# A routed feed-forward behind normalised attention: the last token chunk's dense product on two column halves, with the issue order drawn up anew

## The chip, the cores and the metric

The kernel runs on one core of a Trainium2 chip. The metric is the device time of one execution in microseconds; the profiled execution is recorded by the hardware profiler. The engines are named as in the profile: PE (the matrix engine, with PEld for its weight loads), DVE (vector), ACT (scalar), POOL (gpsimd) and SP (here only a queue that issues DMAs).

## The reference

Eight batches, 12 heads, 448 tokens, head size 64. Attention with normalised q and k gives x, one row of 768 for each of the 3584 tokens; each row then takes a dense feed-forward and one of eight experts.

```python
q_n, k_n = rmsnorm(q, g_q), rmsnorm(k, g_k)
attn = softmax(q_n @ k_n.T / 8)
x = (attn @ v) as rows [3584, 768]

y_dense = maximum(x @ w1_dense, 0) @ w2_dense      # 768 -> 512 -> 768
logits = x @ w_gate                                # 8 experts
e = argmax(logits); gate = softmax(logits)[e]
y_moe = gate * (maximum(x @ w1[e], 0) @ w2[e])
out = y_dense + y_moe
```

## The kernel before

The attention works in 24 groups of four heads, three groups to a batch, so a batch is one round of the steady state. Per group there are seven score steps (`scores`, L339 on PE, two heads at a time on two row halves of 64; then one exponential of 128x896 on ACT, L341), the product with v (`attend`, L357), transposes of q and k (`transposes`, L304), their copies out of PSUM on DVE (qT L317, kT L323 and L325), the division (L390, L384), the transposes of x (`xtrans`, L398) and the gate logits (L416). The norms go through DVE statistics (L272), small ACT steps (m L279, ln L285, r L287) and POOL (ss L281, then four multiplications xn, L293). POOL also casts v (`values`, va, L258), issues the weight loads (L629) and the scatters.

When a batch of x is done, its 448 tokens are taken in four chunks of 128 columns that begin at 0, 128, 256 and 320 (`QC`), so that the first 64 rows of the last chunk repeat the third one's. For each chunk m, `dense` multiplies x by `wd1` (six matmuls of 128x512, L572), `relu` (L576, ACT) writes the result as bf16 beside x in the token's record, and `scatter` (L477, POOL) sends the 128 records to a slot in DRAM. The slots come from `choose`, `ranks` (L463) and `places`: `places` multiplies the ranks by the one-hot choice (at, L471), sums over eight experts (sf, L473) and adds `inval` (L474), which is zero but for the first 64 rows of the last chunk, where it is so large that the scatter skips the repeated rows.

From about 206 us on the kernel is in its tail: records are read back sorted by expert, transposed by DMA (`turn`, on SP), in tiles of 128 tokens. Each tile takes `gemm1` (L762), a transpose (`htrans`, L777), and `gemm2` (L790 for the dense second matrix, L801 for the expert's), a copy out (L814) and a scatter of the output (L817). A few tiles hold two experts with 64 tokens each. Their matmuls work on two column halves of the array (L758 with L759, L801 with L806): 64 stationary columns each, the two results in partitions 0 to 63 and 64 to 127. The dense products of batches 6 and 7 partly lie between the first tiles.

The order on every engine is fixed by hand. The dictionary `AT` gives each step of the steady state a place in units of score steps; all steps are sorted by it and issued in that order, and each engine works through its share in order. `AT["pro"]` and `AT["tail"]` list the start and the tail step by step; `AT["we"]` gives places to weight loads by number (17 is the first matrix of the last expert), and `AT["wt"]` can put such a load ahead of a tile of the tail.

Of the kernel before, what the change touches and what calls it, by code (L numbers as in the profile page):

```python
# [17 lines left out]
AT = dict(  # L18
    p00=[-0.862, 1.524, -1.092],
    p01=[1.061, 2.118, -0.075],  # L20
    d0=[1.097, 3.011, 0.182],
    p10=[3.67, 3.575, 2.886],
    p11=[4.686, 3.605, 4.04],
    d1=[7.184, 5.02, 4.162],
    xt=[11.96, 12.342, 14.734],
    xe=[12.836, 12.616, 15.279],
    tr=[2.755, 1.399, 2.327],
    tq=[3.163, 3.396, 3.158],
    tk=[3.197, 4.021, 5.092],
    va=[-0.884, 1.723, 1.392],  # L30
    st=[(0.275, 0.047), (-0.382, 0.169), (-0.631, 0.101)],
    me=[2.591, 2.79, 3.569],
    no=[3.342, 3.796, 4.041],
    nm=[(7.457, 0.108), (4.843, 0.142), (5.124, 0.082)],
    kq='qk',
    lv=[-8.965, -4.183, -6.466],
    lq=[6.473, 4.67, 2.212],
    lk=[4.188, -0.439, 2.722],
    lo=[13.905, 13.666, 16.642],
    ch=(10.029, 0.135),  # L40
    ra=11.951,
    pl=(13.119, 0.051),
    ga=(10.595, 0.157),
    de=[(0, 0, [(11.866, 0, 4), (12.291, 4, 6)], 13.185, 14.228),
        (1, 1, [(14.061, 0, 2), (14.676, 2, 6)], 14.828, 20.5),
        (2, 0, [(20.56, 0, 6)], 20.943, 27.29), (3, 0, [(26.48, 0, 6)], 28.824, 32.5)],
    we={1: 16.0, 2: 122.0, 3: 20.0, 4: 32.85, 5: 45.7, 6: 58.55, 7: 71.4, 8: 84.25, 9: 97.1,
        10: 109.95, 11: 122.8, 12: 135.65, 13: 139.5, 14: 144.215, 15: 145.293, 16: 150.009, 17: 212.877, 18: 160.695},
    bl=24.0,
    wt={},  # L50
    el=(146.335, 0.654),
    s0=[-0.586, 0.455, 2.566],
    s1=[-2.814, 1.363, 3.272],
    s2=[0.964, 2.804, 2.08],
    s3=[0.9, 0.991, 3.16],
    s4=[3.908, 5.032, 3.847],
    s5=[5.085, 6.201, 1.162],
    s6=[5.915, 4.026, 6.263],
    pro=[('ld', 'k', 0), ('ld', 'q', 0), ('id',), ('ld', 'q', 1), ('gl',), ('co',),
# [23 lines left out]


@with_exitstack
def kernel(
# [73 lines left out]
    dbase = const.tile([P, 4], F32)  # L160
    inval = const.tile([P, 4], F32)
    oh = const.tile([P, B + 1, 5, E], BF16)
# [207 lines left out]
    def free(who):  # L370
        for p in [p for p in held if held[p] == who]:
            del held[p]
# [196 lines left out]
    def dense(b, m, bank, k0, k1):  # L569
        claim("0" if bank == 0 else "1 1r", ("de", b, m))  # L570
        for kk in range(k0, k1):
            seen(nc.tensor.matmul(W[:, bank], xTs[b][:, kk, QC[m]:QC[m] + P], wd1[:, kk],  # L572
                             start=(kk == 0), stop=(kk == KD - 1)), "W", "pe", bank)

    def relu(b, m, bank):
        seen(nc.scalar.activation(rb[b % 3][:, m, XH:GO].bitcast(BF16), W[:, bank], AF.Relu),  # L576
             "W", "act", bank)
        free(("de", b, m))
# [3 lines left out]
    def constants():  # L582
        nc.vector.memset(ones, 1.0)
        nc.vector.memset(onef, 1.0)
        nc.vector.memset(inval, 0.0)
        nc.vector.memset(inval[:D, 3:4], OOB)
        for e in range(E):
# [56 lines left out]
    def attention():  # L644
# [30 lines left out]
        for b in range(B):  # L675
            z = J * NB * (b + 1)
            put(at("ch", z, 0), ("ch", b), 8, lambda b=b: choose(b))
            put1(at("ra", z, 0), ("ra", b), ranks, b)
            put(at("pl", z, 0), ("pl", b), 3, lambda b=b: places(b))
# [283 lines left out]
```

## Time and profile before

| what | value |
|---|---|
| median of 3 runs | 355.06 us |
| lowest and highest of the 3 | 354.93, 364.9 us |
| the profiled execution's own time | 355.05 us |
| its span, first to last instruction | 353.4 us |
| busy: PE, DVE, ACT, POOL | 321.0, 220.2, 212.8, 203.5 us |
| granted TensorE clock, mean | 0.994 |

A busy PE includes the latency of its matmuls, so the pitch at which matmuls follow one another says more of its load than its busy share. In rows of the timeline a name such as L572 is the line in the kernel, then operation, tile written and tile read, shape and count; a bracket at the end gives the idle time of the engine just before and what ended it.

### The profile page before, as it was taken

To read this page: it belongs to the slowest core of one execution; us is meant where nothing else is said; L and a number is where in the kernel's file an instruction comes from. 1 tells how busy PE (TensorE), PEld (TensorE's weight loads), DVE (VectorE), ACT (ScalarE), POOL (GpSimd) and SP (SyncE) were. 2 spreads that over 40 slices of the span, in tenths; PEclk is the share of its full clock that TensorE was granted. 3 is DMA by queue.
4 is the path that set the end of the run, shared out by engine and by line. 5 is a ranking of instruction groups with operands and counts; after the bars stand their busy time and mean duration, and the time that the engine had idled before them with its cause. 6 is when DMAs were issued, how large, how long until landed. Compare 5 with 4: busy or idle time off the path is not lost.

```text
span 353.4 us, 11109 instructions
## 1 busy us (share of the span) xinstructions
PE 321.0 (91%) x4058; PEld 194.4 (55%) x4058; DVE 220.2 (62%) x801; ACT 212.8 (60%) x342; POOL 203.5 (58%) x282
## 2 busy tenths in 40 slices
PE   0498989999999999999998998999999999999991
PEld 0255655666565665666565565555555555555550
DVE  4978999989889888898987734362222222442321
ACT  2379998798898997988987733322233222332220
POOL 4476897697896987988989321555232222222321
PEclk9999999999999999999999999999999999999997
DMA  7996999999999999969999998999966666666312
GB/s 234 234 267 182 290 268 275 294 244 307 274 309 288 243 318 263 295 185 285 295 243 217 246 196 173 209 282 263 259 172 166 185 185 167 159 155 146 104 67 91
DMA packets 81817, 79.80 MB, mean 226 GB/s; under 512 B 48222, under 2 KB 73310, under 8 KB 81760
## 3 DMA queue, kind: packets, MB, share of 16 engines
q1 hardware_dynamic: 70672, 43.24, 49.0%
q0 software_dynamic: 11088, 35.80, 37.7%
q8 instruction: 36, 0.59, 0.7%
q14 instruction: 21, 0.17, 0.2%
HBM read 61.40 MB, written 24.07 MB: 242 GB/s over the span
## 4 chain that ended last, share of the span: by engine, by line
PE 21%; issue 19%; DMA 10%; POOL 6%; ACT 5%; POOLq 3%; DVE 2%; DVEq 0%; ACTq 0%
DMA out_dram<-xflat,tail 9%; PE W L572 7%; PE AV L357 5%; POOL out_dram L817 4%; ACT xflat L341 4%; PE sc L339 3%; POOLq L816 1%; DMA xflat<-records 1%; PE W L398 1%; PE W L304 1%; POOL xn L293 1%; POOLq L562 1%; PE mid L762 1%; PE yp L790 1%; PE AV L416 1%
## 5 line engine op out<-in xcount | busy, mean ns | idle before, releaser
L341 ACT ACTIVATE xflat<-sc 128x896 bf16<-128x896 f32 x168 | 144.6, 917 | 13.5 <-PE sc L339 12.2
L293 POOL TENSOR_TENSOR xn<-we,r 128x448 bf16<-128x448 f32 x92 | 83.9, 944 | 14.2 <-ACT r L287 6.9
L357 PE MATMUL AV<-va,xflat 128*128 128x65 bf16 (+1 forms) x1536 | 75.9, 195 | 1.7 <-issue 0.7
L814 DVE COPY xflat<-yp 128x768 f32<-128x768 f32 x29 | 27.7, 956 | 78.5 <-PE yp L801 68.6
L817 POOL DMA_INDIRECT out_dram<-xflat,tail x30 | 30.9, 1031 | 78.3 <-DVE xflat L814 64.3
L339 PE MATMUL sc<-qT,kT 64*128 64x448 bf16 x384 | 68.0, 366 | 7.2 <-ACT xflat L341 4.8
L357 PEld LDWEIGHTS <-xflat 128*128 128x128 bf16 (+1 forms) x1536 | 60.1, 97 | 25.4 <-issue 14.4
L272 DVE BATCH_NORM_STATS2 st<-we 128x6 f32<-128x128 f32 x336 | 69.8, 279 | 2.8 <-DMA we<-in_k_dram 2.8
L781 ACT COPY heT<-AV 128x512 bf16<-128x512 bf16 x27 | 15.8, 586 | 56.3 <-PE AV L777 56.3
L572 PE MATMUL W<-wd,xT 128*128 128x512 bf16 x192 | 47.5, 380 | 1.0 <-DVE kT L325 1.0
L477 POOL DMA_INDIRECT records<-rall,slot x32 | 33.3, 1040 | 25.4 <-DVE rall L450 7.3
L801 PE MATMUL yp<-we,heT 128*128 (+1 forms) x240 | 44.0, 326 | 0.0
L790 PE MATMUL yp<-wd,xflat 128*128 128x384 bf16 x240 | 43.9, 326 | 0.0
L384 DVE TENSOR_TENSOR rall<-AV,inv 128x256 bf16<-128x256 f32 x96 | 36.3, 420 | 2.0 <-DVE inv L390 0.3
L339 PEld LDWEIGHTS <-kT 64*128 64x128 bf16 x384 | 24.1, 95 | 22.8 <-issue 17.3
L762 PE MATMUL W<-we,xflat 128*128 x144 | 35.0, 379 | 0.7 <-issue 0.7
L790 PEld LDWEIGHTS <-xflat 128*128 128x128 bf16 x240 | 23.2, 98 | 18.9 <-issue 1.2
L767 ACT ACTIVATE hs<-W,tail 128x512 bf16<-128x512 f32 x27 | 18.6, 687 | 23.5 <-PE W L762 16.3
L801 PEld LDWEIGHTS <-heT 128*128 128x128 bf16 (+1 forms) x240 | 23.4, 99 | 15.6 <-issue 1.0
L576 ACT ACTIVATE rall<-W 128x512 bf16<-128x512 f32 x32 | 19.0, 597 | 19.5 <-PE W L572 19.4
L258 POOL CAST va<-we 128x448 bf16<-128x448 f32 x48 | 26.9, 590 | 0.0
L572 PEld LDWEIGHTS <-xT 128*128 128x128 bf16 x192 | 16.4, 97 | 19.0 <-issue 3.8
(132 smaller groups left out, 301.4 us busy)
## 6 DMA issues: line engine op xcount, KB each, us to landing
we<-in_moe_w_dram POOLq DMA_DIRECT2D x16, 768.0 KB
we<-in_q_dram SPq DMA_DIRECT2D x24, 448.0 KB
we<-in_k_dram SPq DMA_DIRECT2D x11, 896.0 KB
we<-in_v_dram SPq DMA_DIRECT2D x48, 128.0 KB
we<-in_v_dram SPq DMA_DIRECT2D x48, 96.0 KB
wd<-in_moe_w_dense_dram POOLq DMA_DIRECT2D x2, 768.0 KB
records<-rall POOLq DMA_DIRECT2D x8, 162.0 KB
we<-in_k_dram SPq DMA_DIRECT2D x2, 448.0 KB
```

Source lines behind the costliest of these rows:

```text
L272: return [lambda s=s: nc.vector.bn_stats(sts[g][:, "qk".index(name), s].rearrange("p h c -> p (h c)"), xin[name, g].rearrange("p h (s d) - ...
L293: (eng or nc.gpsimd).tensor_tensor(xn[name, g][:, :, hh], xin[name, g][:, hh].rearrange("p (s d) -> p s d", d=D), r[:, "qk".index(name), : ...
L339: nc.tensor.matmul(ps[:, hh, :S], kT[row, c:c + P], qT[row, r], start=(n == 0), stop=(n == len(mm) - 1), skip_group_check=True)
L341: nc.scalar.activation(x, ps[:, :, :S], AF.Exp, scale=scale)
L357: seen(nc.tensor.matmul(av[:, hh, m], exs[g, s][rows_, hh, QC[m]:QC[m] + P], va[rows_, s, hh, :De], start=(first and s == full[0] and m == ...
L384: seen(nc.vector.tensor_tensor(x[:, 2 * hh + r], av[:, hh, :, :D].rearrange("p m (a i) -> p m a i", a=2), inv[:, hh].unsqueeze(3).to_broad ...
L477: i = nc.gpsimd.indirect_dma_start(out=rec, out_offset=bass.IndirectOffsetOnAxis(ap=slot[b % 2][:, m:m + 1], axis=0), in_=rb[b % 3][:, m], ...
L572: seen(nc.tensor.matmul(W[:, bank], xTs[b][:, kk, QC[m]:QC[m] + P], wd1[:, kk], start=(kk == 0), stop=(kk == KD - 1)), "W", "pe", bank)
L762: got = [nc.tensor.matmul(he, xRs[t][:, kk], w, **args)]
L790: nc.tensor.matmul(yps[t][:, dd, :HD], xRs[t][:, KD + i], wd2[:, i, dd * HD:(dd + 1) * HD], start=(i == 0), stop=False, skip_group_check=True)
L801: done.append(nc.tensor.matmul(yp[:cut, dd, :HD], heTs[t][:, i, :cut], mats(t)[:, bass.ds(eregs[t], 1), 1, cols] .rearrange("p o f -> p (o ...
L817: i = nc.gpsimd.indirect_dma_start(out=out, out_offset=bass.IndirectOffsetOnAxis(ap=tail[:, t, 1:2], axis=0), in_=ys.rearrange("p a d -> p ...
```

## The change

Four things change. First, `dense` for the last chunk (m = 3) takes only the 64 new tokens as stationary columns, and computes the 512 outputs as two halves of 256, one on each column half of the array: twelve matmuls of 64x256 in place of six of 128x512. `relu` for that chunk becomes two activations of 64x256, which both write to partitions 64 to 127; the other 64 records of that chunk are zeroed once at the start. Second, `places` keeps `inval` as a ninth column of its product tile, so that one sum over nine columns writes the slot. Third, all numbers in `AT` are new, which moves steps on every engine. Fourth, weight load 17 leaves the list of the tail and goes ahead of tile 5 on POOL.

```diff
-    de=[(0, 0, [(11.866, 0, 4), (12.291, 4, 6)], 13.185, 14.228),
-        (1, 1, [(14.061, 0, 2), (14.676, 2, 6)], 14.828, 20.5),
-        (2, 0, [(20.56, 0, 6)], 20.943, 27.29), (3, 0, [(26.48, 0, 6)], 28.824, 32.5)],
+    de=[(0, 0, [(11.933, 0, 4), (12.358, 4, 6)], 12.949, 14.283), (1, 1, [(14.061, 0, 2), (14.379, 2, 6)], 14.828, 20.5), (2, 0, [(20.557, 0, 6)], 20.995, 27.068), (3, 0, [(26.48, 0, 6)], 28.938, 32.5)],
...
-    wt={},
+    wt={5: [17]},
...
-          ('g2', 0, 1), ('we', 17), ('tu', 2), ('de', 7, 2), ('re', 7, 2), ('se', 7, 2),
...
     def places(b):
         rk = W[:, 1, RK:].rearrange("p (m e) -> p m e", e=E)
-        at = sb.tile([P, 4, E], F32, tag="at", name="at")
-        sf = sb.tile([P, 4], F32, tag="sf", name="sf")
-        return [lambda: (seen(nc.vector.tensor_tensor(at, rk, oh[:, b, :4], ALU.mult), "W", "dve", 1),
-                         free(("ra", b))),
-                lambda: nc.vector.tensor_reduce(sf, at, AX.X, ALU.add),
-                lambda: nc.vector.tensor_tensor(slot[b % 2], sf, inval, ALU.add)]
+        at = ats[b % 2]
+
+        def found():
+            with nc.allow_low_precision(reason="whole numbers, at most one of them not zero"):
+                nc.vector.tensor_reduce(slot[b % 2], at, AX.X, ALU.add)
+
+        return [lambda: (seen(nc.vector.tensor_tensor(at[:, :, :E], rk, oh[:, b, :4], ALU.mult),
+                              "W", "dve", 1), free(("ra", b))), found]
...
         for kk in range(k0, k1):
-            seen(nc.tensor.matmul(W[:, bank], xTs[b][:, kk, QC[m]:QC[m] + P], wd1[:, kk],
-                             start=(kk == 0), stop=(kk == KD - 1)), "W", "pe", bank)
+            if m < 3:
+                seen(nc.tensor.matmul(W[:, bank], xTs[b][:, kk, QC[m]:QC[m] + P], wd1[:, kk],
+                                 start=(kk == 0), stop=(kk == KD - 1)), "W", "pe", bank)
+                continue
+            for h in range(2):
+                seen(nc.tensor.matmul(W[h * D:(h + 1) * D, bank, :F // 2], xTs[b][:, kk, S - D:],
+                                 wd1[:, kk, h * F // 2:(h + 1) * F // 2], start=(kk == 0),
+                                 stop=(kk == KD - 1), skip_group_check=True), "W", "pe", bank)
...
+        out = rb[b % 3][:, m, XH:GO].bitcast(BF16)
+        if m < 3:
+            seen(nc.scalar.activation(out, W[:, bank], AF.Relu), "W", "act", bank)
+        else:
+            for h in range(2):
+                seen(nc.scalar.activation(out[D:, h * F // 2:(h + 1) * F // 2],
+                                          W[h * D:(h + 1) * D, bank, :F // 2], AF.Relu),
+                     "W", "act", bank)
...
+        for at in ats:
+            nc.vector.memset(at[:, :, E:], 0.0)
+            nc.vector.memset(at[:D, 3, E:], OOB)
+        nc.vector.memset(rall[:D, 3:12:4, XH:GO], 0.0)
```

Three places in the order matter for what follows. On PE, in the middle of a round of the steady state, behind the transposes of x (L398) and one score step: sc, AV and W are PSUM tiles, xT is the transposed x. Before:

```order
L398 LDWEIGHTS rall
L398 MATMUL W<-ident,rall 128x128
L339 LDWEIGHTS kT_88
L339 MATMUL sc<-qT,kT_88 128x448
L339 LDWEIGHTS kT_88
L339 MATMUL sc<-qT,kT_88 128x448
L357 LDWEIGHTS xflat
L357 MATMUL AV<-va_90,xflat 128x65
```

and now:

```order
L396 LDWEIGHTS rall
L396 MATMUL W<-ident,rall 128x128
L337 LDWEIGHTS kT_89
L337 MATMUL sc<-qT,kT_89 128x448
L337 LDWEIGHTS kT_89
L337 MATMUL sc<-qT,kT_89 128x448
L573 LDWEIGHTS xT
L573 MATMUL W<-wd_86,xT 128x512
```

The dense product of chunk 2 (six matmuls) now stands directly behind the score step; the 16 matmuls of `attend` that stood between them follow later.

On ACT, near the end of a round, from the ln and r steps on (rall is the record, W the dense product). Before:

```order
L285 ACTIVATE ln<-ss,eps_t 128x28
L287 ACTIVATE r<-ln 128x28
L341 ACTIVATE xflat<-sc 128x896 x3
L576 ACTIVATE rall<-W 128x512
L341 ACTIVATE xflat<-sc 128x896 x3
L279 ACTIVATE m_3731<-st 128x28
```

and now:

```order
L283 ACTIVATE ln<-ss,eps_t 128x28
L285 ACTIVATE r<-ln 128x28
L339 ACTIVATE xflat<-sc 128x896 x4
L587 ACTIVATE rall<-W 64x256 x2
L339 ACTIVATE xflat<-sc 128x896 x2
L277 ACTIVATE m_3715<-st 128x28
```

The relu of chunk 3 is two instructions and stands behind one exponential more.

On POOL, two groups of one round of the steady state. Before:

```order
L281 TENSOR_TENSOR ss<-st,m_2729 128x28
L293 TENSOR_TENSOR xn<-we,r 128x7x64 x4
L477 DMA records<-rall,slot_81 29824x648
L629 DMA we<-in_moe_w_dram 128x3072
L258 CAST va_91<-we 128x2x7x32 x2
L281 TENSOR_TENSOR ss<-st,m_2907 128x28
L477 DMA records<-rall,slot_81 29824x648
L293 TENSOR_TENSOR xn<-we,r 128x7x64 x4
```

and now:

```order
L279 TENSOR_TENSOR ss<-st,m_2740 128x28
L256 CAST va_92<-we 128x2x7x32 x2
L291 TENSOR_TENSOR xn<-we,r 128x7x64 x4
L477 DMA records<-rall,slot_82 29824x648
L643 DMA we<-in_moe_w_dram 128x3072
L279 TENSOR_TENSOR ss<-st,m_2888 128x28
L291 TENSOR_TENSOR xn<-we,r 128x7x64 x4
L477 DMA records<-rall,slot_82 29824x648
```

The cast of v moved ahead of the first group's xn, and the scatter moved behind the second group's xn.

## Rows read from the trace of the kernel before

**Rows 1.** Busy time by stretch: us, PE, PEld, DVE, ACT, POOL busy, clock, DMA share, GB/s.

```profile
160.00:170.00 10.00, 9.96 (x157) 5.98 (x154) 8.93 (x35) 9.03 (x17) 9.21 (x13) 1.00 1.11 264
206.00:236.00 30.00, 28.46 (x213) 16.03 (x211) 13.39 (x59) 9.16 (x16) 11.99 (x16) 1.00 1.00 206
```

**Rows 2.** ACT's timeline, one step per batch that marks the round: start, length, what.

```profile
127.05 0.23 ACT L448 ACTIVATE eg<-cent 128x32 f32<-128x32 f32 x1
...
151.79 0.23 ACT L448 ACTIVATE eg<-cent 128x32 f32<-128x32 f32 x1
...
175.49 0.23 ACT L448 ACTIVATE eg<-cent 128x32 f32<-128x32 f32 x1
...
201.40 0.24 ACT L448 ACTIVATE eg<-cent 128x32 f32<-128x32 f32 x1
```

**Rows 3.** Chain that ended last, around one product of chunk 3: start, length, what.

```profile
168.22 1.40 PE W L572 x6
...
170.78 0.59 ACT rall L576
171.37 2.44 ACT xflat L341 x3
...
173.85 0.37 PE sc L339 x2
```

**Rows 4.** ACT's timeline, the relu of one chunk 2, with its wait in brackets.

```profile
163.78 0.60 ACT L576 ACTIVATE rall<-W 128x512 bf16<-128x512 f32 x1 [0.86 <-PE W L572]
```

**Rows 5.** PE's timeline: a tile with two experts on column halves, then an ordinary one.

```profile
304.08 0.39 PE L777 MATMUL AV<-ident,hs 128*128 128x128 bf16 x4
304.40 0.40 PE L758 MATMUL W<-we,xflat 128*64 x1
304.40 0.40 PE L759 MATMUL W<-rall,xflat 128*64 128x512 bf16 x1
...
305.50 0.38 PE L758 MATMUL W<-we,xflat 128*64 x1
...
305.82 1.47 PE L790 MATMUL yp<-wd,xflat 128*128 128x384 bf16 x8
...
308.43 0.39 PE L777 MATMUL AV<-ident,hs 128*128 128x128 bf16 x4
308.65 1.46 PE L762 MATMUL W<-we,xflat 128*128 x6
```

**Rows 6.** PE's timeline at the start of the tail.

```profile
206.10 4.05 PE L572 MATMUL W<-wd,xT 128*128 128x512 bf16 x18
...
212.37 1.46 PE L762 MATMUL mid<-we,xflat 128*128 x6 [0.62 <-DMA records<-rall,slot]
```

**Rows 7.** Groups by line: busy us, mean ns | idle before.

```profile
L576 ACT ACTIVATE rall<-W 128x512 bf16<-128x512 f32 x32 | 19.0, 597 | 19.5 <-PE W L572 19.4
...
L474 DVE TENSOR_TENSOR slot<-sf,inval 128x4 int32<-128x4 f32 x8 | 4.5, 567 | 0.3
...
L448 ACT ACTIVATE eg<-cent 128x32 f32<-128x32 f32 x8 | 1.8, 231 | 0.0
...
L473 DVE TENSOR_REDUCE sf<-at 128x4 f32<-128x32 f32 x8 | 1.5, 186 | 0.3
```

**Rows 8.** POOL's timeline in the round from 127 us on, and in the tail.

```profile
135.37 0.25 POOL L281 TENSOR_TENSOR ss<-st,m 128x28 f32<-128x28 f32 x1 [0.69 <-ACT m L279]
137.06 3.64 POOL L293 TENSOR_TENSOR xn<-we,r 128x448 bf16<-128x448 f32 x4 [1.45 <-ACT r L287]
...
141.88 1.11 POOL L258 CAST va<-we 128x448 bf16<-128x448 f32 x2
...
144.43 1.02 POOL L477 DMA_INDIRECT records<-rall,slot  x1 [0.30 <-ACT ln L285]
145.47 3.64 POOL L293 TENSOR_TENSOR xn<-we,r 128x448 bf16<-128x448 f32 x4
...
223.77 0.83 POOL L629 DMA_DIRECT2D we<-in_moe_w_dram  x1
```

More of the change, by code (lines that the diff above doesn't have):

```diff
@@ L18 @@
 AT = dict(
[L19 to L34, printed above, removed]
+    p00=[1.034, 1.637, -1.254],
+    p01=[0.933, 2.118, -0.422],
+    d0=[1.862, 3.175, 0.182],
+    p10=[3.354, 3.452, 1.559],
+    p11=[4.623, 3.764, 4.04],
+    d1=[7.422, 5.376, 4.044],
+    xt=[12.229, 12.171, 12.814],
+    xe=[13.191, 12.774, 15.097],
+    tr=[3.037, 1.439, 2.838],
+    tq=[3.331, 1.483, 4.496],
+    tk=[3.484, 2.462, 3.101],
+    va=[-0.443, -3.08, 1.359],
+    st=[(-0.738, 0.047), (-0.382, 0.205), (-0.631, 0.101)],
+    me=[2.381, 2.625, 3.368],
+    no=[3.397, 3.831, 4.146],
+    nm=[(5.662, 0.106), (5.074, 0.072), (5.102, 0.087)],
     kq='qk',
@@ L38 @@
     lk=[4.188, -0.439, 2.722],
[L39 to L43, printed above, removed]
-    de=[(0, 0, [(11.866, 0, 4), (12.291, 4, 6)], 13.185, 14.228),
-        (1, 1, [(14.061, 0, 2), (14.676, 2, 6)], 14.828, 20.5),
-        (2, 0, [(20.56, 0, 6)], 20.943, 27.29), (3, 0, [(26.48, 0, 6)], 28.824, 32.5)],
+    lo=[13.313, 13.584, 16.691],
+    ch=(10.096, 0.135),
+    ra=12.215,
+    pl=(13.157, 0.01),
+    ga=(10.805, 0.171),
+    de=[(0, 0, [(11.933, 0, 4), (12.358, 4, 6)], 12.949, 14.283), (1, 1, [(14.061, 0, 2), (14.379, 2, 6)], 14.828, 20.5), (2, 0, [(20.557, 0, 6)], 20.995, 27.068), (3, 0, [(26.48, 0, 6)], 28.938, 32.5)],
     we={1: 16.0, 2: 122.0, 3: 20.0, 4: 32.85, 5: 45.7, 6: 58.55, 7: 71.4, 8: 84.25, 9: 97.1,
-        10: 109.95, 11: 122.8, 12: 135.65, 13: 139.5, 14: 144.215, 15: 145.293, 16: 150.009, 17: 212.877, 18: 160.695},
+         10: 109.95, 11: 122.8, 12: 135.65, 13: 139.5, 14: 144.215, 15: 145.293, 16: 150.009,
+         18: 160.695},
     bl=24.0,
-    wt={},
+    wt={5: [17]},
     el=(146.335, 0.654),
[L52 to L58, printed above, removed]
+    s0=[-0.963, 0.743, 2.604],
+    s1=[-2.076, 2.06, 3.295],
+    s2=[1.364, 2.693, 2.08],
+    s3=[0.93, 0.991, 2.948],
+    s4=[3.908, 5.389, 3.864],
+    s5=[4.974, 5.762, 0.631],
+    s6=[5.606, 4.369, 6.052],
     pro=[('ld', 'k', 0), ('ld', 'q', 0), ('id',), ('ld', 'q', 1), ('gl',), ('co',),
@@ L160 @@
     dbase = const.tile([P, 4], F32)
-    inval = const.tile([P, 4], F32)
+    ats = [const.tile([P, 4, E + 1], F32, name=f"at{i}") for i in range(2)]
     oh = const.tile([P, B + 1, 5, E], BF16)
@@ L571, in dense @@
         for kk in range(k0, k1):
-            seen(nc.tensor.matmul(W[:, bank], xTs[b][:, kk, QC[m]:QC[m] + P], wd1[:, kk],
-                             start=(kk == 0), stop=(kk == KD - 1)), "W", "pe", bank)
-    def relu(b, m, bank):
-        seen(nc.scalar.activation(rb[b % 3][:, m, XH:GO].bitcast(BF16), W[:, bank], AF.Relu),
-             "W", "act", bank)
+            if m < 3:
[6 more added lines that the diff above has]
+                                 stop=(kk == KD - 1), skip_group_check=True), "W", "pe", bank)
+    def relu(b, m, bank):
+        out = rb[b % 3][:, m, XH:GO].bitcast(BF16)
[6 more added lines that the diff above has]
+                     "W", "act", bank)
         free(("de", b, m))
@@ L584, in constants @@
         nc.vector.memset(onef, 1.0)
-        nc.vector.memset(inval, 0.0)
-        nc.vector.memset(inval[:D, 3:4], OOB)
+        for at in ats:
+            nc.vector.memset(at[:, :, E:], 0.0)
+            nc.vector.memset(at[:D, 3, E:], OOB)
+        nc.vector.memset(rall[:D, 3:12:4, XH:GO], 0.0)
         for e in range(E):
@@ L678, in attention @@
             put1(at("ra", z, 0), ("ra", b), ranks, b)
-            put(at("pl", z, 0), ("pl", b), 3, lambda b=b: places(b))
+            put(at("pl", z, 0), ("pl", b), 2, lambda b=b: places(b))
             put(at("ga", z, 0), ("ga", b), 4, lambda b=b: gates(b))
```

10 rows, old and new, of the table tail are left out of this document.

## The prediction

> **What bounds the kernel now.** I read the busy time by stretch first. In the steady state PE, DVE, ACT and POOL are all busy nine tenths of the time [rows 1], and in the first 30 us of the tail PE is busy for 28.46 of 30.00 us while the others fall to half or less. So the tail is PE's, and what is taken from PE there is gained, but for the waits on data. In the steady state no engine has room of its own, and the question is which wait ends last. The step that marks a round [rows 2] gives the periods: 24.74, 23.70 and 25.91 us between its last four starts, so the same work takes a lean round or one about 1 us longer, and the last also holds the list for the tail.
>
> The chain of waits [rows 3] shows the end of a lean round. PE comes first: six matmuls of chunk 3 in 1.40 us. Then ACT takes over: the relu and three exponentials run without a gap from 170.78 us, and PE's next score step starts only at 173.85. So right behind chunk 3 ACT, not PE, sets the pace, while earlier in the round ACT waits for PE, as at the relu of chunk 2, which sat idle for 0.86 us until the dense product ended [rows 4]. The two hand the round to each other.
>
> **Chunk 3 on column halves.** A pair of 64-column matmuls is in the trace already, in the tail's tiles with two experts [rows 5]. Both members start at 304.40 us, and the first members of the six pairs go from 304.40 to 305.50, a pitch of 0.22 us. That is the pitch of one full matmul of 512 columns: 1.40 us for six [rows 3], or 4.05 us for eighteen with the latency of the last [rows 6]. So the halves do run beside each other. With 256 columns in place of 512 a pair should take between 0.108 us (half the pitch) and 0.216 us (no overlap). I take 0.108, since the rows show full overlap. Six steps then take 0.65 us where they took 1.30, a gain of 0.65 us per batch.
>
> The switch of shape costs something. Into the halves PE goes 0.32 us after the transposes, where an ordinary tile follows after 0.22 (308.43 to 308.65); out of them it takes 0.32 in place of 0.22. That is 0.10 each way. In six of the eight batches chunk 3 stands between score steps, which use row halves, and already pays one such switch: 1.40 us for six where the pitch says 1.30. There I add nothing. In the tail (batches 6 and 7) the neighbours are full matmuls, so each product gains 0.65 - 0.20 = 0.45 us, or 0.9 us for the two. Of this the wait of 0.62 us before the first tile [rows 6] may swallow the first half, since that tile waits for records; so the tail's term lies between 0.45 and 0.9, and I take 0.9 because that tile's records too leave earlier if the steady state is shorter. On the six in the steady state 3.9 us of PE time fall away, and how much reaches the end is the main question: nothing if ACT holds the round, all if ACT is relieved as well.
>
> The Trainium skill, page "TensorEngine Tiling (Array Packing)", section "Tiling Modes", states that changing the tiling mode drains the engine. The trace agrees, with the 0.10 us each way above. The sum would be the same without this sentence. The same page's "Restrictions and Gotchas" states that column tiling goes without fast weight loads. No row shows a pair of only 256 columns; if loads then held a pair at the 512 pitch, the gain would be nil, which is the rival of halves that don't pay.
>
> **What ACT pays and gets.** The relu of chunk 3 becomes two. A straight line through 231 ns for 32 columns and 597 ns for 512 [rows 7] gives an estimate of 402 ns for 256, so 0.80 in place of 0.60 us: 0.20 us more per batch, at most, on an engine that sets the pace there. Against it stands the new order on PE: chunk 2's product comes directly behind a score step instead of behind 16 matmuls of the attention product. ACT's relu then finds it done sooner, and of the 0.86 us wait [rows 4] most should go. Net, ACT gets up to 0.86 - 0.20 = 0.66 us per round, about what PE gets. As the two hand the round to each other, a round can shorten by 0 to 0.65 us. I take 0.5, nearer the top since both are relieved by the same size: 6 x 0.5 = 3.0 us.
>
> **POOL's new order.** In the longer round POOL's four multiplications started at 145.47 us, behind a scatter that took 1.02 us from 144.43 [rows 8]; PE's transposes wait for them. That scatter is now behind the multiplications. The gain is bounded by what the longer round has over the lean one, 24.74 - 23.70 = 1.04 us [rows 2], in three rounds or so: 0 to 3.1 us. Part of that is the same time as the term above, so I take 0.6 us. The cast of v moves ahead of the first group's multiplications. It takes 1.11 us, and POOL idled for 1.45 us at that very place waiting for ACT's r, so I cost it at nothing; if that wait is gone the cast delays them by its full length (below).
>
> **The smaller parts.** The slot's sum drops an instruction of 567 ns mean; the sum over nine columns should take the 186 ns of the sum over eight [rows 7]. That frees about 0.57 us of DVE per batch, off the path by the rows 3, and the scatter behind it leaves that much earlier. I count 0, between 0 and 0.2 us for each of six rounds. The memset of the unused records stands at the start, where DVE has nothing until the first k arrives: 0. Weight load 17 takes POOL 0.83 us at 223.77 [rows 8]; moved behind, it lets two scatters and the fill of gaps go earlier, and PE loses 1.54 of 30 us in that stretch in all [rows 1]. I count 0, and from 0.7 us gained to 1 us lost if the load then comes in the way of tile reads.
>
> **The sum.** The profiled execution took 355.05 us, the median of the runs is 355.06, so no correction is needed. 355.05 - 0.9 - 3.0 - 0.6 = 350.55; I predict 350.5 us, a gain of 1.3%. Less than 2% can't be told from no change with this measurement.
>
> **Rivals.**
> The round doesn't shorten. ACT is busy 9.03 of 10 us and POOL 9.21 [rows 1], and right behind chunk 3 ACT runs without a gap [rows 3]. If ACT's extra 0.20 us and its dependence on score steps hold the round, only the tail's 0.9 us is left: 354.1 us. For it speaks the gapless stretch, against it that ACT waits elsewhere for PE. Chance 0.2. The Trainium skill, same page, section "Performance Considerations", gives this as a rule: tiling speeds TensorE but not the reading out of PSUM, which may become the bottleneck. That rule would give this rival's time.
>
> All of it is gained: 0.65 in six rounds, 0.9 in the tail, 2.5 to 3.1 on POOL, 0.5 from the weight load. 355.05 - 3.9 - 0.9 - 2.8 - 0.5 = 346.95 us, with 346 to 348 around it. All engines being relieved at once speaks for it, the overlap of the terms against it. Chance 0.15.
>
> The halves don't pay: a pair takes the pitch of 512. Then the two tail products lose 0.20 us each, ACT 0.20 per round, and the new order gives some 0.6 to 1.5 us back: about 355 us. Rows 5 speak against it. Chance 0.05.
>
> Slower: the cast ahead of the multiplications. If ACT's r is ready as soon as POOL reaches them (the wait of 1.45 us [rows 8] under 1.11 in the new order), each round starts its transposes late by up to 1.11 us. PE and ACT then wait on POOL: 7 x 1.11 = 7.8 us, less the tail's 0.9: 361.9 us at full price, 358 at half. It decides from the point where the wait there falls below the cast's length; as PE and ACT get quicker the wait should shrink, but the load and scatter behind it moved away too. Chance 0.04.
>
> **How the numbers follow.** The forecast has 0.56, with a range of its own from 348.5 to 352.5. The range for 8 in 10 takes in most of the full gain and the round that doesn't shorten: 346.8 to 354.4. Faster by over 2% means under 347.95: two thirds of the full gain and a little of the forecast's low end, 0.12. Slower by over 2% means over 362.15: 0.02. Within: 0.86.
>
> **What would show it.** In the changed trace the twelve small matmuls should start in pairs at about 0.11 us, some 0.75 us per product with the switch; the two small relus at about 0.4 us each; chunk 2's relu with little wait; rounds of 23.1 to 23.8 us, with the longer kind nearly gone; the slot's sum near 0.19 us. I am wrong if pairs don't overlap, if rounds stay at 23.7 and 24.7 (ACT holds), if POOL's first multiplications of a round start behind the cast with PE waiting for them, or if the first expert tiles wait longer for their records or for weight load 17.

## The result, and the profile after

The changed kernel took 355.67 us (median of 21 runs) beside 357.39 us for the kernel before (21 runs). In both kernels a part of the runs is several us slower, and the ratio compares only the others, so it is not the quotient of these medians. The ratio is 0.9898 with a 95% interval of 0.9865 to 0.9931: of 355.05 us that is 3.6 us less, between 2.4 and 4.8. It is a gain, and smaller than the 2% that is called a change here. The forecast of 350.5 us is a ratio of 0.987, inside the interval.

The profiled execution of the changed kernel took 360.37 us, since PE waited 5.66 us for the records of one tile at 262.32 us and had a mean granted clock of 0.66 between 260 and 270 us (partly at 1.2 GHz); so its timeline is read here only up to 215 us, and a repeat of the same kernel (e1_again, 352.92 us) stands in for the tail.

PE's timeline of the changed kernel at the start of the tail answers to [rows 6], and L577 is the product on column halves:

```profile
204.49 2.78 PE L573 MATMUL W<-wd,xT 128*128 128x512 bf16 x12
207.20 0.85 PE L577 MATMUL W<-wd,xT 128*64 128x256 bf16 x12
207.98 1.49 PE L355 MATMUL AV<-va,xflat 128*128 128x65 bf16 x32
...
210.57 1.46 PE L776 MATMUL mid<-we,xflat 128*128 x6 [0.81 <-DMA records<-rall,slot]
```

Twelve small matmuls take 0.85 us to the end of the last and 0.78 to the next instruction. From the first dense matmul to the attention product is 207.98 - 204.49 = 3.49 us, where eighteen full ones take 3.89 us (e2_no_halves below, 210.74 to 214.63): 0.40 us less. The wait of 0.62 us before the first tile is now 0.81 (0.70 in e1_again).

ACT's timeline, the mark of four rounds, answers to [rows 2]:

```profile
125.46 0.25 ACT L446 ACTIVATE eg<-cent 128x32 f32<-128x32 f32 x1
150.24 0.25 ACT L446 ACTIVATE eg<-cent 128x32 f32<-128x32 f32 x1
174.48 0.25 ACT L446 ACTIVATE eg<-cent 128x32 f32<-128x32 f32 x1
199.82 0.23 ACT L446 ACTIVATE eg<-cent 128x32 f32<-128x32 f32 x1
```

Rounds of 24.78, 24.24 and 25.34 us: the long kind is not gone. The chain that ended last, around chunk 3 in the first of these rounds, a long one, answers to [rows 3]:

```profile
145.16 0.93 ACT xflat L339
...
146.12 0.38 ACT rall L587
...
146.50 0.38 ACT rall L587
...
146.91 0.93 ACT xflat L339
147.83 0.04 issue
147.88 0.55 PE sc L337 x4
```

PE's product of chunk 3 has left the chain here. ACT holds it from an exponential through both small relus, one behind the other, until PE's next score step.

The groups by line answer to [rows 7] (L584 the full relu, L587 the small ones); under it DVE's timeline with the slot's sum and xT's copy behind it:

```profile
L584 ACT ACTIVATE rall<-W 128x512 bf16<-128x512 f32 x24 | 14.3, 597 | 14.1 <-PE W L573 11.8 <-issue 2.0
L587 ACT ACTIVATE rall<-W 64x256 bf16<-64x256 f32 x16 | 6.0, 377 | 1.8 <-issue 1.5
```
```profile
152.72 0.19 DVE L471 TENSOR_REDUCE slot<-at 128x4 int32<-128x36 f32 x1
152.83 0.61 DVE L402 COPY xT<-W 128x896 bf16<-128x896 bf16 x1
```

POOL's timeline in the same round answers to [rows 8]:

```profile
133.88 0.24 POOL L279 TENSOR_TENSOR ss<-st,m 128x28 f32<-128x28 f32 x1 [0.77 <-ACT m L277]
134.07 1.11 POOL L256 CAST va<-we 128x448 bf16<-128x448 f32 x2
135.50 3.64 POOL L291 TENSOR_TENSOR xn<-we,r 128x448 bf16<-128x448 f32 x4 [0.32 <-issue]
...
143.01 3.63 POOL L291 TENSOR_TENSOR xn<-we,r 128x448 bf16<-128x448 f32 x4 [0.53 <-DMA we<-in_v_dram]
146.81 1.04 POOL L477 DMA_INDIRECT records<-rall,slot  x1 [0.17 <-issue]
```

The cast fits into the wait for r, and the scatter stands behind the multiplications, both as planned; yet this round took 24.78 us.

### The profile page after: what moved, and what is told of

It reads as the page before. It is cut to its first block, busy times and chain, and to the rows that moved or that the text cites. A ratio compares the mean times of both kernels' runs of the same rounds, so it can differ in the third digit from the quotient of the medians.

```text
span 358.7 us, 11206 instructions
## 1 busy us (share of the span) xinstructions
PE 317.9 (89%) x4106; PEld 195.5 (55%) x4106; DVE 215.9 (60%) x796; ACT 215.8 (60%) x350; POOL 203.7 (57%) x282
## 4 chain that ended last, share of the span: by engine, by line
PE 33%; DMA 21%; issue 20%; ACT 9%; DVE 7%; POOL 6%; POOLq 2%; SPq 2%; DVEq 0%
DMA out_dram<-xflat,tail 8%; PE AV L355 8%; ACT xflat L339 7%; PE W L573 7%; PE sc L337 6%; DMA we<-in_v_dram 6%; DMA we<-in_k_dram 4%; POOL out_dram L831 3%; DVE st L270 2%; PE yp L804 2%; PE yp L815 2%; PE W L302 2%; POOL xn L291 2%; PE W L396 2%; POOLq L830 1%
## 5 line engine op out<-in xcount | busy, mean ns | idle before, releaser
L337 PE MATMUL sc<-qT,kT 64*128 64x448 bf16 x384 | 71.1, 367 | 10.7 <-ACT xflat L339 7.5
L804 PE MATMUL yp<-wd,xflat 128*128 128x384 bf16 x240 | 45.2, 333 | 0.0
L776 PE MATMUL W<-we,xflat 128*128 x144 | 36.2, 389 | 6.3 <-DMA xflat<-records 5.7
L573 PE MATMUL W<-wd,xT 128*128 128x512 bf16 x144 | 36.2, 380 | 0.0
L804 PEld LDWEIGHTS <-xflat 128*128 128x128 bf16 x240 | 23.5, 99 | 19.8 <-issue 3.0
L776 PEld LDWEIGHTS <-xflat 128*128 128x128 bf16 x162 | 15.2, 99 | 21.5 <-DMA xflat<-records 5.7
L302 PE MATMUL W<-ident,xn 64*128 64x64 bf16 x672 | 16.2, 195 | 11.2 <-POOL xn L291 10.9
```

Of the source, the lines that this page charges most:

```text
L337: nc.tensor.matmul(ps[:, hh, :S], kT[row, c:c + P], qT[row, r], start=(n == 0), stop=(n == len(mm) - 1), skip_group_check=True)
L776: got = [nc.tensor.matmul(he, xRs[t][:, kk], w, **args)]
L804: nc.tensor.matmul(yps[t][:, dd, :HD], xRs[t][:, KD + i], wd2[:, i, dd * HD:(dd + 1) * HD], start=(i == 0), stop=False, skip_group_check=True)
```

## The experiments

All are variants of the changed kernel, but for e3_halves_only and e12_before_less_load, which are made from the kernel before. From each profile come the starts of the six steady rounds. The second round came out at 23.45 to 23.50 us in all six profiles with the changed order, halves and places, so it compares the order on the engines; the sum of six includes what waits for data cost in that execution. No ratio is on record for e2_no_halves.

| kernel | median us (runs) | ratio to before, 95% | second round us | sum of six us |
|---|---|---|---|---|
| before | | | 23.71 | 147.23 |
| changed | 355.67 (21) | 0.990 (0.987 to 0.993) | 23.49 | 146.45 |
| e1_again | 358.83 (12) | 0.993 (0.987 to 1.000) | 23.45 | 146.57 |
| e8_again2 | 355.0 (6) | 0.988 (0.983 to 0.992) | 23.48 | 146.19 |
| e4_load17_back | 350.94 (6) | 0.984 (0.976 to 0.992) | 23.46 | 142.32 |
| e7_load17_back2 | 358.94 (6) | 0.987 (0.981 to 0.993) | 23.50 | 149.26 |
| e2_no_halves | 358.34 (6) | none | 23.65 | 152.70 |
| e9_halves_tail | 354.45 (4) | 0.989 (0.980 to 0.997) | 23.65 | 143.29 |
| e3_halves_only | 356.73 (12) | 0.998 (0.994 to 1.003) | 23.94 | 148.48 |
| e6_relu_one | 357.31 (6) | 0.996 (0.990 to 1.002) | 23.05 | 146.44 |
| e5_relu_dve | 369.23 (6) | 1.034 (1.029 to 1.038) | 26.11 | 163.59 |
| e10_old_places | 362.58 (6) | 1.017 (1.008 to 1.026) | 24.09 | 153.36 |
| e11_changed_less_load | 362.74 (4) | 1.018 (1.012 to 1.025) | 23.46 | 142.34 |
| e12_before_less_load | 359.35 (4) | 1.011 (1.002 to 1.020) | 23.71 | 144.65 |

The medians scatter more than the second rounds do, so the verdicts below rest on rows and take the ratios as support.

### The halves, in the rounds and in the tail

e1_again and e8_again2 are the changed kernel without an edit.

> The changed kernel once more, for an undisturbed profile and as the yardstick of this group. The step that marks a round (the small exponential of the gates, 128x32) went from 147.2 us between its first and its seventh start to 146.5 us in the one profile seen so far. Theory (ACT holds the end of each round): that stays, the six rounds together are 0 to 1.5 us shorter than before, the start up to the first mark about 0.8 us shorter, and the tail about 1 us shorter; in all 351 to 352.5 us. Rival (the rounds did shorten as predicted, by about 0.5 us each, and the one profile seen was disturbed there too): rounds of 144 us or less from first to seventh mark.

> The changed kernel a third time, beside the one with load 17 in its old place. Theory (load 17 is neutral): its undisturbed runs lie at 347 to 351 us, as with the load in its old place; a profile shows rounds of 23.46 us except where DVE waits for a k load. Rival (the load's new place costs): 351 us and more in every run, with the loss behind tile 5 of the tail.

Both profiles have the lean round of 23.45 to 23.48 us, but the forecasts held only in part. In e1 the six rounds are 0.66 us shorter than before and the start 0.55 us, while the tail is not 1 us shorter: from the first tile to the start of the last eight matmuls it took 131.68 us, 131.71 before. The three quickest runs of e8 took 351.56 to 352.57 us, above the 347 to 351 of its theory; its tail took 131.55 us, so no loss behind tile 5 explains them, and its rounds of 24.81 and 24.22 us come without a long wait of DVE for a load of k, as the section on the long rounds shows.

e2_no_halves takes the halves out and keeps the new order:

```diff
-            if m < 3:
-                seen(nc.tensor.matmul(W[:, bank], xTs[b][:, kk, QC[m]:QC[m] + P], wd1[:, kk],
...
+            seen(nc.tensor.matmul(W[:, bank], xTs[b][:, kk, QC[m]:QC[m] + P], wd1[:, kk],
...
-            for h in range(2):
-                seen(nc.scalar.activation(out[D:, h * F // 2:(h + 1) * F // 2],
...
+        seen(nc.scalar.activation(rb[b % 3][:, m, XH:GO].bitcast(BF16), W[:, bank], AF.Relu),
```

> The changed kernel with the dense product and the relu of the last chunk as before (six matmuls of 128x512, one relu), all else as changed. Theory (in the rounds the PE time that the halves free is lost again at ACT, whose two small relus take 0.77 us where one took about 0.5 of pitch; only the tail keeps the gain): rounds from first to seventh mark within 0.7 us of the changed kernel, the tail 0.8 us longer, so 0.3 to 1.5 us slower than the changed kernel and still faster than before. Rival (the halves carry the gain, the new order is only fitted to them): 3 us or more slower than the changed kernel, back at the time before.

e9_halves_tail keeps them for the last two batches alone:

```diff
-            if m < 3:
+            if m < 3 or b < B - 2:
...
-        if m < 3:
+        if m < 3 or b < B - 2:
```

> The column halves are kept for the last two batches alone, whose dense product lies in the tail; the six in the rounds take six matmuls of 128x512 and one relu again, in the new order. Theory A (in a round the two small relus give back nearly all that the twelve narrow matmuls free, so a round is only 0.2 us shorter with the halves): the undisturbed rounds are 23.65 us in place of 23.45, the way from the seventh mark to the first tile stays at 10.6 to 10.8 us, and the whole is 1.2 us longer than the changed kernel. Theory B (the halves in a round are worth 0.5 us, as the prediction had it): rounds of 23.95 us and 3 us longer. Theory C (the halves only cost time in the rounds): rounds of 23.3 us or less, and up to 1 us shorter than the changed kernel.

Both gave rounds of 23.65 to 23.66 us, three of the six in each, where the changed kernel's lean rounds are 23.45 to 23.50. So in the new order the halves are worth 0.19 us per round, as theory A of e9 had it, and not 0.5. (Its other forecast missed: the way from the seventh mark to the first tile was 11.65 us, since the first tile waited 1.70 us for its records.) ACT's timeline shows why. First e9, with chunk 2's relu, which waits for nothing, and then the one full relu behind chunk 3:

```profile
135.81 0.60 ACT L584 ACTIVATE rall<-W 128x512 bf16<-128x512 f32 x1
...
140.38 0.23 ACT L285 ACTIVATE r<-ln 128x28 f32<-128x28 f32 x1
140.51 1.71 ACT L339 ACTIVATE xflat<-sc 128x896 bf16<-128x896 f32 x2
142.70 1.76 ACT L339 ACTIVATE xflat<-sc 128x896 bf16<-128x896 f32 x2 [0.48 <-PE sc L337]
144.36 0.59 ACT L584 ACTIVATE rall<-W 128x512 bf16<-128x512 f32 x1
144.84 1.73 ACT L339 ACTIVATE xflat<-sc 128x896 bf16<-128x896 f32 x2
```

and the same place with the halves (e11_changed_less_load, whose lines stand one further down):

```profile
124.79 0.23 ACT L286 ACTIVATE r<-ln 128x28 f32<-128x28 f32 x1
124.92 3.34 ACT L340 ACTIVATE xflat<-sc 128x896 bf16<-128x896 f32 x4
128.28 0.77 ACT L588 ACTIVATE rall<-W 64x256 bf16<-64x256 f32 x2
129.07 1.73 ACT L340 ACTIVATE xflat<-sc 128x896 bf16<-128x896 f32 x2
```

With the full product ACT waits 0.48 us for the score step that PE issues behind it. With the halves that wait is gone, but the two relus take 0.79 us to the next exponential where the one took 0.48: from r to that exponential 4.28 us in place of 4.46. So ACT gains 0.48 us and pays 0.31 of it back.

PE's side of the same two rounds says the same. The product takes 1.40 us to the next score step in e9 (from 140.89 us) and 0.78 in e11 (from 125.31), so 0.62 us fall away. Some 5 us later PE waits for ACT, first e9, then e11:

```profile
145.81 0.55 PE L337 MATMUL sc<-qT,kT 64*128 64x448 bf16 x4 [0.22 <-ACT xflat L339]
```
```profile
130.04 0.55 PE L338 MATMUL sc<-qT,kT 64*128 64x448 bf16 x4 [0.66 <-ACT xflat L340]
```

Of the 0.62 us, 0.44 go into this longer wait, and 0.18 are left, the 0.19 of the round.

e3_halves_only adds the halves to the kernel before, with its order and its places:

```diff
+            for h in range(2):
+                seen(nc.tensor.matmul(W[h * D:(h + 1) * D, bank, :F // 2], xTs[b][:, kk, S - D:],
+                                 wd1[:, kk, h * F // 2:(h + 1) * F // 2], start=(kk == 0),
...
+            for h in range(2):
+                seen(nc.scalar.activation(out[D:, h * F // 2:(h + 1) * F // 2],
...
```

> The kernel before with nothing but the halves of the last chunk (twelve matmuls, two relus, the zeroed records). Theory (ACT holds the end of each round): rounds from first to seventh mark 147 us, give or take 0.8, so unchanged or a little longer for the second relu; tail 0.8 us shorter; in all 0.3 to 1.5 us faster than before. Rival (PE holds the rounds): 0.65 us less per round, 143.3 us from first to seventh mark, and 4 to 5 us faster in all.

In that order ACT already ran gapless behind the relu [rows 3], so there was no wait to remove: the second round is 23.94 us against 23.71, longer by 0.23, somewhat less than the 0.31 of the second relu, and the kernel as a whole shows no gain (ratio 0.998). So the two parts need each other: the halves alone cost a round 0.23 us, the new order alone (e2, e9) saves some 0.05, and together they save 0.25.

e6_relu_one takes one relu of 128x256 in place of the two and leaves out the move of the two halves side by side, so the dense part of those records is wrong; e5_relu_dve gives the second small relu to DVE:

```diff
-            for h in range(2):
-                seen(nc.scalar.activation(out[D:, h * F // 2:(h + 1) * F // 2],
...
+            seen(nc.scalar.activation(out[:, :F // 2], W[:, bank, :F // 2], AF.Relu),
+                 "W", "act", bank)
```
```diff
-            for h in range(2):
-                seen(nc.scalar.activation(out[D:, h * F // 2:(h + 1) * F // 2],
...
+            seen(nc.scalar.activation(out[D:, :F // 2], W[:D, bank, :F // 2], AF.Relu),
+                 "W", "act", bank)
+            seen(nc.vector.tensor_scalar(out[D:, F // 2:], W[D:, bank, :F // 2], 0.0, None,
+                                         op0=ALU.max), "W", "dve", bank)
```

> The changed kernel with one relu of 128x256 in place of the two of 64x256 for the last chunk. It leaves out the move of the two halves side by side, so the dense part of those records is wrong; the work on PE is the changed kernel's. Theory (ACT holds the end of a round): an undisturbed round of 23.05 to 23.25 us, since about 0.38 us of ACT go. Rival (the relus are hidden): 23.4 to 23.5 us.

> The changed kernel with the second of the two small relus of the last chunk on DVE instead of ACT. Theory (ACT holds the end of a round: 23.46 us with the halves, 23.66 with whole matmuls and one relu): taking 0.38 us off ACT there shortens an undisturbed round to 23.1 to 23.3 us, 1 to 2 us over six rounds. Rival (what holds the round's end is PE's score steps or DVE, not the relus): the round stays at 23.4 to 23.5 us, or grows by what DVE waits for the dense product.

With one relu the second round was 23.05 us, 0.41 less, the length of the relu that is gone (377 ns), as its theory had it. The other five were 23.47 to 25.63 us, so this rests on one round. On DVE, against the theory, the relu costs far more than it saves, 25.17 to 26.11 us in the middle four rounds: its instruction stands in DVE's order and waits there for ACT's half, with DVE's other work behind it:

```profile
105.51 0.43 DVE L588 TENSOR_SCALAR rall<-W 64x256 bf16<-64x256 f32 x1 [1.15 <-ACT rall L586]
```

### Weight load 17

e4_load17_back and, once more on another chip, e7_load17_back2 put the load back to its place in the tail's list:

```diff
-         18: 160.695},
+         17: 212.877, 18: 160.695},
...
-    wt={5: [17]},
+    wt={},
```

> The changed kernel with the last expert's first matrix loaded where it was before, between two steps of the tail's list. Theory (PE sets the tail, POOL has room there): within 0.5 us of the changed kernel. Rival (the load's 0.8 us on POOL and its traffic held the first tiles): the expert tiles behind the list start 0.7 to 1.5 us later against the first tile than in the changed kernel, and the time is as much longer.

> The changed kernel with load 17 back in its old place, a second time, beside the changed kernel on one chip. Theory (load 17 is neutral; the first time the rounds were undisturbed by chance, for the rounds lie before either place of the load): the undisturbed profile has rounds of 23.46 us as in the changed kernel and the same length from the first tile to the last matmul, and the times of the two spread over the same 347 to 361 us. Rival (the load's new place costs): the changed kernel's undisturbed runs are again 2 us or more slower than this one's.

e4 was the fastest kernel of all. Its profiled execution of 348.4 us was 4.52 us shorter than e1's, but 4.25 us of that lie in the six rounds, which both kernels issue alike and which end before either place of the load. From the first tile to the start of the last eight matmuls it took 131.50 us, e1 131.68, e8 131.55, the kernel before 131.71. The same kernel as e7 had rounds that sum to 149.26 and a tail of 135.84 us, in which one tile waited 3.27 us for its records; the changed kernel's own profile has such a wait of 5.66 us. Side by side on one chip the two places gave ratios of 0.987 (e7) and 0.988 (e8). So the load's place makes no difference that these runs show, and e4's lead was in what happened to be late.

### The long rounds

In one round what was late is plain: e1's fifth, of 27.63 us, where DVE's timeline has a wait for a load of k that e4's, in a round of 23.68, hardly has:

```profile
155.15 1.85 DVE L270 BATCH_NORM_STATS2 st<-we 128x6 f32<-128x128 f32 x9 [3.90 <-DMA we<-in_k_dram]
```
```profile
151.74 1.87 DVE L270 BATCH_NORM_STATS2 st<-we 128x6 f32<-128x128 f32 x9 [0.48 <-DMA we<-in_k_dram]
```

Two kernels test whether the weights that are loaded in the rounds cause it. Both leave six of the sixteen expert loads out and zero that memory once at the start, which moves the first mark some 7 to 8 us later, so rounds are compared:

```diff
+    nc.vector.memset(we[:, 2:5], 0.0)
...
-            put1(t, ("we", n), nc.gpsimd.dma_start, *wjobs[n])
+            if n not in range(7, 13):
+                put1(t, ("we", n), nc.gpsimd.dma_start, *wjobs[n])
```

> The changed kernel without the six weight loads of experts 2, 3 and 4; their place in memory is set to zero once at the start by DVE, so the output is not the reference's. Theory A (the long rounds of the changed kernel come from loads of k and v that share the DMA engines with the weights): from the fourth round on every round takes 23.4 to 23.7 us, no wait of over 1 us for in_k or in_v, the six rounds sum to 140.5 to 142.5 us. Theory B (the long rounds come from the order on the engines): rounds of 24.2 to 25.3 us remain and the sum stays at 145 us or more. The first mark may come some us later by the zeroing, so the rounds are compared and not the whole time.

> The kernel before without the same six weight loads, zeroed in the same way. If the long rounds of before are the loads' too (theory A), its rounds fall to 23.7 us and the sum of six from 147.2 to 142 to 143.5, and the changed kernel's lead over it in the rounds is 0.2 to 0.3 us each, 1.5 us in all. If they are the order's own (theory B), rounds of 24.5 to 25.9 us remain, the sum stays at 146 to 147 us, and the lead is 4 us or more.

In rounds two to five theory A held for both: those of the changed kernel were 23.46, 23.47, 23.45 and 23.47 us, those of the kernel before 23.71, 23.68, 23.70 and 23.69. The sixth, which also holds the list for the tail, took 24.52 and 24.76. For e12 two figures missed: the sum of 144.65 us lies above 142 to 143.5, for the first round stayed at 25.11, and the changed kernel's lead is 2.31 us, not 1.5. The windows show the DMA engines (the columns are start and end, then length, busy PE, PEld, DVE, ACT, POOL, clock, DMA share, GB/s): e11, e12, a 24.8 us round of e8_again2, and the fourth round of e1_again, with all its loads:

```profile
132.41:155.86 23.45, 22.68 (x413) 14.83 (x414) 20.79 (x85) 21.71 (x37) 19.14 (x27) 1.00 0.81 252
```
```profile
133.48:157.18 23.70, 23.59 (x410) 14.85 (x406) 21.22 (x86) 21.33 (x37) 19.19 (x27) 1.00 0.76 243
```
```profile
124.70:149.50 24.80, 23.28 (x416) 15.25 (x415) 20.88 (x85) 21.88 (x37) 20.62 (x28) 1.00 1.07 295
```
```profile
124.58:148.03 23.45, 22.68 (x414) 14.82 (x414) 20.78 (x85) 21.71 (x37) 20.63 (x29) 1.00 1.08 284
```

Without the six loads the DMA share is 0.75 to 0.82 in rounds three to five, and all of them are lean. But the share does not tell a long round from a lean one: at 1.08 e1's took 23.45 us, at 1.07 e8's took 24.80. Nor is a late load seen in the rounds of 24.8 us (the changed kernel's and e8's fourth): no wait for a load is longer there than 0.86 us, beside 0.78 in e1's lean fourth. What starts late is DVE's first copy of qT, 8.3 us into the round in place of 7.4, though PE's transposes for it start 6.46 us into the round in the changed kernel's profile and in e1's alike; what it waited for is not shown. So a late load is shown as the cause of e1's fifth round. That the weight loads cause the other long rounds is supported by e11 and e12, one profile each, whose four times lie within 2.2 and 4.0 us of each other where the 21 of the changed kernel lie within 10; it is not shown, since e4, with every load of the rounds, ran rounds two to five at 23.45 to 23.68 us too.

Per round (the fourth of e11 and of e12) PE is busy 0.91 us less and ACT 0.38 us more than before, and the round is 0.25 us shorter: the gain on PE is there, and waits for ACT take most of it.

These two runs give the rounds with no long one among them: 142.34 - 144.65 = -2.31 us in the six, of which 1.14 in the first (23.97 against 25.11), 0.93 in the next four and 0.24 in the last. With all loads the sums were 2.6 us higher for the kernel before and 3.9 to 4.2 higher in three profiles of the changed one, though not at all in e4. Why one execution is hit and another is not stays open.

As whole kernels the two go the other way: e11 took 362.74 us and e12 359.35 (medians of four). In its profile e11 has its first mark 0.53 us later than e12, needs 13.50 us in place of 10.78 from the seventh mark to the first tile, which waits 3.56 us for its records, and then 134.25 in place of 131.39 to the last eight matmuls. Waits of 1.7 us and more for the records of a tile also stand in the profiles of the changed kernel, e3, e7, e9 and e10, so in both orders and with load 17 in either place, and in none of before, e1, e2, e4, e8 and e12. What decides them is open; where they come, they take more than the rounds have gained.

The runs also show that the scatter in front of the multiplications does not by itself make a long round. In e12 it still stands there, as in [rows 8], and the round is lean (the view ends within the fourth multiplication):

```profile
149.44 0.99 POOL L478 DMA_INDIRECT records<-rall,slot  x1 [0.16 <-ACT xflat L342]
150.47 2.74 POOL L294 TENSOR_TENSOR xn<-we,r 128x448 bf16<-128x448 f32 x3
```

### The slots by one sum

e10_old_places puts the former three steps back into the new order:

```diff
-                nc.vector.tensor_reduce(slot[b % 2], at, AX.X, ALU.add)
...
+                lambda: nc.vector.tensor_reduce(sf, at, AX.X, ALU.add),
+                lambda: nc.vector.tensor_tensor(slot[b % 2], sf, inval, ALU.add)]
```

> The changed kernel with the slots by the former three steps (product, sum over eight columns, one addition). Theory A (DVE has room at that place, the prediction's term of 0): undisturbed rounds of 23.4 to 23.5 us and a time within 0.5 us of the changed kernel. Theory B (the step removed stands on the way to the scatters): rounds longer by 0.06 to 0.2 us, 0.4 to 1.2 us in all.

This was the surprise. The second round is 24.09 us (the first and fourth 24.10 and 24.09), 0.63 longer than with the sum, beyond theory B's upper end of 0.2, and the kernel is 1.7% slower than before. DVE's timeline of e10 in two rounds, then POOL's of the same two:

```profile
104.68 3.18 DVE L472 TENSOR_TENSOR slot<-sf,inval 128x4 int32<-128x4 f32 x1
107.78 0.61 DVE L402 COPY xT<-W 128x896 bf16<-128x896 bf16 x1
...
157.55 0.90 DVE L472 TENSOR_TENSOR slot<-sf,inval 128x4 int32<-128x4 f32 x1
158.38 0.61 DVE L402 COPY xT<-W 128x896 bf16<-128x896 bf16 x1
...
209.79 0.16 DVE L472 TENSOR_TENSOR slot<-sf,inval 128x4 int32<-128x4 f32 x1
```
```profile
103.17 3.63 POOL L291 TENSOR_TENSOR xn<-we,r 128x448 bf16<-128x448 f32 x4
106.75 1.08 POOL L256 CAST va<-we 128x448 bf16<-128x448 f32 x2
...
155.70 3.63 POOL L291 TENSOR_TENSOR xn<-we,r 128x448 bf16<-128x448 f32 x4 [0.28 <-issue]
```

The addition of four numbers per partition takes 0.16 us in the tail, where POOL is idle beside it. Beside POOL's multiplications it took 0.90 us, to 158.45: the four of 0.91 us each follow from 155.70, so their third ends at about 158.43. In the other round it lasted until 107.86, past all four multiplications and the two casts that began at 106.75. In the new order xT's copy stands behind it and the gate's matmuls behind that; PE waited 2.85 us for xT there, and the granted clock over 102 to 126 us was 0.86, partly at 1.2 GHz, in a round of 28.79 us. The sum that replaces it runs in 0.19 us beside the same multiplications (152.72 above, with POOL's four from 151.09 to 154.72).

## Why the prediction was right, and where its steps were not

The sign, the size class and the range held, but the sum came out near the result by errors against each other, which is luck. Predicted were 0.9 + 3.0 + 0.6 = 4.5 us, measured 3.6 (2.4 to 4.8).

**Halves in the tail: right mechanism, but the gain is not seen at the end.** The pairs run beside each other, 0.78 us per product with the switches of shape (forecast 0.75). The first product gives 0.40 us for the predicted 0.45. From the seventh mark to the first tile it is 10.97 us before and 10.99 in e2, which has no halves, 10.75 in the changed profile and 10.63 in e1, so 0.2 to 0.35 gets through. The second product's 0.45 does not show: first tile to last eight matmuls is 131.71 us before and 131.68 in e1. Taken together, from the seventh mark to the last eight matmuls, it is 142.68 us before, 142.31 in e1 and 142.26 in e8, but 142.22 in e2. Of the term of 0.9, then, 0 to 0.4 us are left, and no run parts it from nothing.

**Six rounds at 0.5 each: the step that failed.** The prediction counted the wait of 0.86 us at chunk 2's relu [rows 4] as time that ACT would be given, and set 0.65 of PE beside 0.66 of ACT. That wait is indeed gone in lean rounds, but without the halves it is gone too (e9 above), and that round is 23.65 us against 23.68 to 23.71: all that the new order does without the halves comes to some 0.05, for a wait of 0.48 us has come up at the end of the round. What decides is that end, where the halves take the wait away and put a second relu in its place, at 0.31 us and not the 0.20 forecast. So a round gains 0.25 us, six of them 1.5, half of the 3.0. The first rival, that ACT's extra relu holds the round, had the right mechanism and went too far: not nothing, but 0.19 us is left of the halves. Its sentence on the Trainium skill ("TensorEngine Tiling (Array Packing)", section "Performance Considerations", that tiling does not speed the reading out of PSUM) fits the 0.79 us of two relus for the 0.48 of one.

**POOL's new order: not a cause.** The term of 0.6 read the long rounds as the order's, with a scatter ahead of the multiplications. In the changed profile the scatter stands behind and the rounds are still 24.24 to 25.34 us; in e12 it is where it was and rounds two to five are 23.68 to 23.71. What makes the long ones is shown for e1's fifth alone, a late load. The DMA share of 1.11 [rows 1] would not have told it either, since that stretch lies in a lean round of 23.70 us. The rival of the cast ahead of the multiplications did not occur: the cast of 1.11 us ended in the idle time of POOL, which still waited 0.32 us.

**The places at 0: wrong.** The prediction took the mean of 567 ns [rows 7] for the length of the addition; it is 0.16 us of work and the rest a wait for POOL. In rounds two to six of before the addition took 0.43 to 0.45 us, and in e12 such rounds are lean. Around the first mark it was this, DVE's and then POOL's timeline of the kernel before:

```profile
57.30 2.01 DVE L474 TENSOR_TENSOR slot<-sf,inval 128x4 int32<-128x4 f32 x1
59.23 1.85 DVE L272 BATCH_NORM_STATS2 st<-we 128x6 f32<-128x128 f32 x9
```
```profile
56.53 2.75 POOL L293 TENSOR_TENSOR xn<-we,r 128x448 bf16<-128x448 f32 x3
59.22 1.10 POOL L258 CAST va<-we 128x448 bf16<-128x448 f32 x2
```

The addition ends as the multiplications end. That first round is 25.11 us, 25.11 again in e12 and 25.08 in e3, each time with an addition of 2.01 us; with the one sum it is 23.7 to 24.0 us where no load is late. So most of the 1.14 us of the first round, some 0.9, seem to go with this wait; no run changed it alone in the old order, so that part is argued from the rows and not shown. In the new order the sum is what the order stands on: without it a round costs 0.63 us more (e10). The Trainium skill, page "SBUF — State Buffer", section "Who interferes with whom", states that a DVE instruction with two SBUF inputs contends with a GpSimd instruction that reads SBUF, and that a tensor_reduce on trn2 never contends. The traces agree with both: 0.16 us alone, 0.43 to 3.18 beside xn, and 0.19 for the sum. The prediction did not consult it for this step.

**Load 17 at 0 and the memset at 0: nothing speaks against them.** The load showed no difference (e4, e7). The first mark came at 53.37 us with the memset (changed) and at 53.32 without it (e2), though in the old order it came at 54.85 with it (e3) and 54.17 without. In the profiles of the changed kernel and e4 it is 0.2 to 0.8 us earlier than in the one of before, but 0.53 later in e11 than in e12, so no gain at the start is shown.

**The sum by what the runs showed:** 2.3 us in the rounds (e11 against e12) and 0 to 0.4 from the tail's product: 2.3 to 2.7 us, at the lower end of the measured interval. The six rounds gave half of their term and POOL's order none of its own, and some 0.9 us came from a term put at nothing. What the long rounds and the late records add or take in the mean of many executions is not in this sum.

## What to carry to other kernels

When two engines hand a round to each other, look at the idle time in front of the other engine at the very place where the work is saved: it bounds the gain, and what the edit adds to that engine comes off it. An operation whose mean is far above what its size explains is a wait; set its start and end beside the other engines before you price its removal, above all for DVE operations with two SBUF inputs beside POOL. And before a long round is put down to the order, profile the same kernel again: here the same round of the same order took 23.45 us in one execution and 24.8 in another, at the same DMA share.

## What the runs showed of the hardware

The wait of DVE's addition was not always one POOL instruction long. It got in at the boundary between two multiplications at 158.4 us, but stood through all the multiplications that were left at 57.30, and through those and two casts at 104.68, so a run of POOL instructions without a gap can hold it for 2 to 3 us; when it gets in earlier is not shown. And the same instructions, in the same order, gave sums of six rounds between 142.32 us (e4) and 149.26 us (e7), where DVE waited 2.81 and 1.82 us for loads of k in the first and fifth; without six weight loads rounds two to five were equal to 0.03 us in one execution of each kernel.
